# Linear attention and a gated long convolution on one core: keys and queries turned by crossbar transfers

## The chip, the cores and the metric

The kernel runs on one core of one Trainium2 chip. The metric is device time in microseconds (us), the median of several executions. A profile of one execution is taken beside it; its span is a little shorter than the time (280.3 against 282.08 us for the profiled run).

## The reference

Two stages, for 8 batches, 8 heads, a sequence of 576 and a head dimension of 64, with 128 random features. First, attention through positive random features:

```
scale = 1 / sqrt(sqrt(64));  q_s, k_s = q * scale, k * scale
phi(x): h = x @ omega.T - |x|^2 / 2;  exp(h - max(h)) / sqrt(128)
q_p, k_p = phi(q_s), phi(k_s)
kv = k_p^T v   (features x head dim, per batch and head);   z = sum over the sequence of k_p
attn = (q_p kv) / (q_p z + 1e-6)
```

Then its heads are put side by side (x: 576 x 512 a batch), and a gated convolution follows:

```
x1, x2, x3 = split(x @ w_proj)            # 512 -> 3 x 512
x2c = irfft(rfft(x2) * filter_fft), along the sequence
out = (x1 * x2c * x3) @ w_out             # float32, 8 x 576 x 512
```

## The kernel before

All of it is one program with everything in bf16 on TensorE. The sequence of 576 is cut into a main part of 512 (`NT` = 4 tiles of 128 rows) and a rest of 64; the rests of two batches share one tile of 128 rows ("left keys", "left queries", "left out").

**Attention, for each batch b.** GpSimd's queue loads `kn`, `qn` and `vn` (`load_main`, L430), 512 KB each in bf16 after the cast in the transfer, two buffers each. They come with the sequence on the partitions, while the feature matmuls need the head dimension there, so they have to be turned. `turn_keys` (L932) and `turn_queries` (L942) each work on half a batch: `transposes` (L818) runs eight 128x128 transposes on TensorE (matmuls against the identity `ident`) into the one PSUM bank `t`, and one copy takes the eight out of PSUM into half of `kt` or `qt`. Keys are copied by VectorE, queries by VectorE in batches 0 and 1 and by ScalarE from batch 2 on. `kt` and `qt` have one buffer each. Then `key_features` (L860) multiplies `kt` with `om2`, two heads' copies of omega on a block diagonal, and ScalarE's exponential writes `ek`; the stage "queries" does the same for `eqt`. "values" finds the maximum over the features and weighs the values with it; "sums" makes `kv` (with the normaliser as a 65th column), "turn out" multiplies `eqt` with it, normalises, and turns the result again (`turn_back`, into `xt`). For batches from `NS` = 2 on the queries are loaded in four pieces with the heads beside each other in a row of the sequence; batches 0 and 1 have another layout.

**The convolution.** The Fourier transform is a set of matmuls with tables of sines, on thirds of the sequence ("fold", "rest", "forward", "inverse"), the two gates are "gates", the last product "out". Between forward and inverse, the halves of `sp` are exchanged over the partitions by transfers on SyncE's queue (`sw<-sp`, and `xw<-xr` for the rest); that queue also stores the output. The filter's spectrum is made once ("filter") and spread by small transfers (`hps`, `hqs`).

**The order of work.** Nothing is issued as it is written. Each call is recorded by a planner (`Plan`); an operation has a due time, the batch number plus `LEAD` of its stage, plus `SHIFT` for some stages and batches, plus `LEAN` for some stages on some engines. A list scheduler with rough costs (`_cost`, L200) then walks through engines, buffers and transfer lanes (`simulate`) and among the operations that can start within 120 ns takes the one that is due first. The order it finds is issued (`issue`, L371), which is why nearly all rows of the profile stand at line 377. Each engine then works through its own queue in that order, and waits where an operand isn't there yet.

Of the kernel before, what the change touches and what calls it, by code (L numbers as in the profile page):

```python
# [20 lines left out]
P = 128  # L21

LEAD = {
    "filter": -1.47, "fold": 3.3, "forward": 1.54, "gates": 4.97, "inverse": -3.71, "keys": -2.66,
    "left keys": -4.9, "left out": -4.44, "left queries": -2.12, "load filter": -0.67,
    "load k": -2.73, "load kl": -3.56, "load q": -1.37, "load ql": 2.9, "load v": -2.25,
    "load vl": 1.29, "load w0": 1.23, "load w1": -2.06, "load w2": -0.52, "out": 3.79,
    "queries": 1.94, "residues": -0.5, "rest": -1.06, "sines": -0.54, "start": -3.3,
    "sums": -0.38, "tables": -3.64, "turn out": -3.39, "turn queries": -3.76, "values": 1.2,
    "zeros": -4.6,  # L30
}

SHIFT = {
    ("filter", 0): 2.36, ("fold", 2): -2.58, ("fold", 6): -3.0, ("forward", 1): 1.21,
    ("forward", 6): 1.02, ("forward", 7): 2.73, ("gates", 0): -0.44, ("gates", 1): -2.7,
    ("gates", 2): -1.54, ("gates", 6): 0.81, ("gates", 7): -2.03, ("keys", 1): 2.3,
    ("keys", 6): 2.62, ("keys", 7): -0.96, ("left keys", 2): 2.75, ("left out", 1): 2.97,
    ("left queries", 7): 1.34, ("load filter", 0): 0.55, ("load k", 0): 0.68, ("load k", 2): 2.87,
    ("load kl", 0): 1.02, ("load q", 0): 0.44, ("load q", 1): -3.0, ("load q", 2): -1.75,
    ("load ql", 0): -1.55, ("load v", 0): -2.22, ("load v", 1): -2.86, ("load v", 2): 2.32,  # L40
    ("load vl", 0): -1.68, ("load w0", 0): -2.48, ("load w1", 0): 2.15, ("load w2", 0): 0.69,
    ("out", 1): -2.05, ("out", 7): 2.04, ("rest", 1): -1.46, ("sines", 0): 2.98,
    ("start", 0): -2.92, ("sums", 7): 1.33, ("turn out", 0): -1.37, ("turn out", 1): -2.6,
    ("turn out", 2): -2.52, ("turn out", 7): -3.0, ("turn queries", 2): 2.54, ("values", 1): 1.63,
    ("values", 6): 3.0,
}
LEAN = {
    ("filter", "DVE"): -2.97, ("fold", "ACT"): -2.99, ("fold", "DVE"): -0.81,
    ("fold", "PE"): -1.4, ("forward", "ACT"): -3.0, ("forward", "DVE"): 2.93,
    ("forward", "PE"): 2.66, ("gates", "ACT"): -2.82, ("gates", "DVE"): -1.75,  # L50
    ("gates", "PE"): 2.18, ("keys", "DVE"): -2.89, ("keys", "PE"): -2.89,
    ("left keys", "DVE"): -1.5, ("left keys", "PE"): 2.06, ("left out", "ACT"): 2.24,
    ("left queries", "PE"): 1.68, ("out", "PE"): -0.68, ("queries", "ACT"): -1.85,
    ("queries", "PE"): -1.44, ("rest", "DVE"): -2.12, ("rest", "PE"): 2.72,
    ("start", "POOL"): 3.0, ("sums", "PE"): -3.0, ("turn out", "DVE"): 2.67,
    ("turn out", "PE"): 0.88, ("turn queries", "PE"): 0.32,
}

SIZE = {FP32: 4, INT32: 4, BF16: 2, FP16: 2, mybir.dt.uint32: 4}
# [57 lines left out]
class Plan:  # L117
# [82 lines left out]
    def _cost(self, op, eng, name, outs, ins):  # L200
        out = outs[0]
        n = self._free(out)
        if name == "dma_start":
            a = out if out.space != bass.MemoryType.DRAM else ins[0]
            run = a.ap[-1][1] * SIZE[a.dtype]
            rows = a.ap[0][1] * self._free(a) // a.ap[-1][1]
            if eng == "POOL":
                op.busy, op.lat = (880.0 if rows > 600 else 720.0), 3300.0
                op.dma = ("SW", rows * max(run, 166) / 198.0)
            else:  # L210
                op.busy, op.lat = 580.0, 2000.0
                op.dma = ("HW", rows * run / 180.0 / (1 if out.space == bass.MemoryType.DRAM else 4))
            return
        half = all(SIZE[a.dtype] == 2 for a in (out, *ins))
        sbuf = all(a.space != bass.MemoryType.PSUM for a in (out, *ins))
        if eng == "PE":
            m = n / 2.4 + 2.5
            op.lat = op.busy + n / 2.4 + 166.0
            op.busy += m
            return  # L220
        if eng == "DVE":
            if name == "memset":
                busy = n * SIZE[out.dtype] / 4.8 + 5.0
            elif name == "reciprocal":
                busy = 5.8 * n + 78.0
            elif name == "tensor_tensor":
                busy = n / (1.92 if half and sbuf else 0.96) + 68.0
            elif name == "scalar_tensor_tensor":
                busy = n / 0.96 + 130.0
            elif name in ("tensor_copy", "tensor_scalar", "tensor_scalar_mul"):  # L230
                rate = (4 if sbuf else 2) if half else (2 if sbuf else 1)
                if name != "tensor_copy" and not sbuf:
                    rate = 1
                busy = n / (0.96 * rate) + (68.0 if half else 100.0)
            elif name == "reduce_max":
                busy = self._free(ins[0]) / 0.96 + 60.0
            else:
                busy = n / 0.96 + 68.0
            op.busy, op.lat = busy, busy + 82.0
        elif eng == "ACT":  # L240
            busy = n * 0.8333 + (52.0 if not sbuf else 190.0)
            op.busy, op.lat = busy, busy + 107.0
        else:
            op.busy = op.lat = n / 1.2 + 100.0
# [136 lines left out]
def kernel(  # L381
# [11 lines left out]
    nc = Plan(tc.nc, tc)  # L393
# [5 lines left out]
    NS = 2  # L399
# [3 lines left out]
    NPAIR = H // 2  # L403
# [107 lines left out]
    for j in range(2):  # L511
        nc.vector.tensor_scalar_mul(
            out=om2[j * D : (j + 1) * D, j, :], in0=omt[:D, :MF], scalar1=qk_scale
# [34 lines left out]
    residues = {}  # L548
# [364 lines left out]
    def attention():  # L913
        ekl = None
        for i in range(B // 2):
# [5 lines left out]
            for bb in range(2):  # L921
                b = 2 * i + bb
# [3 lines left out]
                qn, kn, vn = (nat_tiles[w, b] for w in "qkv")  # L926


                kt = nc.tile(att, [P, H, 2, P], BF16, name="kt", bufs=1)
                qt = nc.tile(att, [P, NT, NPAIR, P], BF16, name="qt", bufs=1)  # L930

                def turn_keys(g):  # L932
                    transposes(
                        kt[:, 4 * g : 4 * g + 4, :, :].rearrange("p h u c -> p (h u) c"),
                        [
                            kn[:, h, 2 * u2 : 2 * u2 + 2, :].rearrange("p t d -> p (t d)")
                            for h in range(4 * g, 4 * g + 4)
                            for u2 in range(2)
                        ],
                    )  # L940

                def turn_queries(g):  # L942
                    transposes(
                        qt[:, 2 * g : 2 * g + 2].rearrange("p t h c -> p (t h) c"),
                        [
                            qn[:, t, 2 * pr : 2 * pr + 2, :].rearrange("p h d -> p (h d)")
                            for t in (2 * g, 2 * g + 1)
                            for pr in range(NPAIR)
                        ]
                        if b >= NS  # L950
                        else [

                            qn[:, h, 2 * u2 : 2 * u2 + 2, :].rearrange("p t d -> p (t d)")
                            for h in range(4 * g, 4 * g + 4)
                            for u2 in range(2)
                        ],
                        b >= 2,
                    )

                def turn_left(dst, src, scalar=False):  # L960
# [27 lines left out]
                if b == 0:  # L988
                    nc.at("residues", 0)
                    make_residues()  # L990
                    nc.at("zeros", 0)
                    nc.vector.memset(vcl[:], 0.0)
                    nc.vector.memset(eql[:], 0.0)
                nc.at("keys", b)
                ek = nc.tile(att, [P, H, NT, MF], BF16, name="ek", bufs=2)
                for g in range(2):

                    turn_keys(g)
                    for h in (4 * g, 4 * g + 2):
                        key_features(  # L1000
                            ek[:, h : h + 2, :, :].rearrange("p h t m -> p (h t m)"),
                            [kt[:, hh, u2, :] for hh in (h, h + 1) for u2 in range(2)],
                        )
# [20 lines left out]
                    left_keys()  # L1024
                nc.at("turn queries", b)
                for g in range(2):
                    turn_queries(g)
                nc.at("values", b)
                weigh_values()

# [2 lines left out]
                for pr in range(NPAIR):  # L1033
                    ps = two_banks()
                    for j in range(2):
                        nc.tensor.matmul(
                            out=ps[:, j, :],
# [4 lines left out]
                            start=True,  # L1042
# [3 lines left out]
                        out=eqt[:, pr].rearrange("p j t c -> p j (t c)")  # L1046
                        if b >= NS
                        else eqt[:, pr].rearrange("p h (u j) c -> p j (h u) c", j=2),
                        in_=ps[:] if b >= NS else ps[:].rearrange("p j (g c) -> p j g c", c=P),
# [440 lines left out]
```

The softmax here doesn't subtract the row's maximum and nothing guards it: scores larger than these inputs give would overflow.

## Time and profile before

| what | value |
|---|---|
| time, median of 3 | 282.09 us (280.8 to 282.12) |
| span of the profiled execution | 280.3 us |
| TensorE clock granted | 0.998 of full |
| VectorE, ScalarE, GpSimd busy | 229.9, 201.4, 62.5 us |
| packets of GpSimd's transfers | 59,616, 17.31 MB |
| packets of SyncE's transfers | 8,280, 12.75 MB |
| HBM read, written | 34.64 MB, 9.44 MB |

A row of the profile names line, engine, operation, the tile written and the tiles read, the shape and the count; behind the bar stand the busy time in us, the mean of one in ns, then the idle time of the engine just before such an instruction and what ended it. `t<-ident,kn` is a transpose of keys on TensorE, `kt<-t` its copy out of PSUM. PE is TensorE, DVE VectorE, ACT ScalarE, POOL GpSimd. Records of matmuls are longer than the distance from one to the next, since matmuls are pipelined.

### The profile page before, as it was taken

How to read it: one execution, taken by the hardware profiler on the slowest of the kernel's cores; microseconds unless marked ns; L12 is line 12 of the kernel's file. 1: busy time of each engine (PE TensorE's matmuls, PEld its weight loads, DVE VectorE, ACT ScalarE, POOL GpSimd, SP SyncE). 2: the span in 40 equal slices, each digit the busy share in tenths (PEclk: the TensorE clock that was granted, in tenths of full speed). 3: DMA queues.
4: the chain of work that ended last, by engine and by line, in shares of the span. 5: the costliest groups of instructions: out<-in, count | busy, mean ns of one | idle time of the engine just before them, and what ended most of it. 6: DMA issues, size and time to landing. Idle time of an engine off the chain costs nothing.

```text
span 280.3 us, 5836 instructions
## 1 busy us (share of the span) xinstructions
PE 255.7 (91%) x2274; PEld 156.2 (56%) x2274; DVE 229.9 (82%) x501; ACT 201.4 (72%) x309; POOL 62.5 (22%) x86
## 2 busy tenths in 40 slices
PE   0276797999999999999999999999999999999994
PEld 0154554666686765667566565586455555454541
DVE  7879986757969999999999999978999456776840
ACT  1877577798669797889998979948855656464443
POOL 8725766623127310062031000000000000000000
PEclk9999999999999999999999999999999999999999
DMA  7999999999599981369319022003002213033135
GB/s 90 188 201 191 165 199 187 207 185 117 52 167 173 127 107 26 115 84 169 67 26 223 27 77 87 37 21 77 1 2 112 78 39 132 37 115 102 47 116 187
DMA packets 68068, 30.56 MB, mean 109 GB/s; under 512 B 39499, under 2 KB 62536, under 8 KB 68040
## 3 DMA queue, kind: packets, MB, share of 16 engines
q0 software_dynamic: 59616, 17.31, 60.0%
q1 hardware_dynamic: 8280, 12.75, 14.6%
q8 instruction: 18, 0.29, 0.4%
q10 hardware_dynamic: 144, 0.13, 0.1%
q14 instruction: 10, 0.08, 0.1%
HBM read 34.64 MB, written 9.44 MB: 157 GB/s over the span
## 4 chain that ended last, share of the span: by engine, by line
PE 65%; DMA 17%; issue 9%; POOL 4%; DVE 3%; ACT 0%; DVEq 0%; POOLq 0%
PE h L377 49%; PE a L377 11%; PE t L377 5%; DMA vn<-in_v_dram 5%; DMA vl<-in_v_dram 5%; DMA ql<-in_q_dram 4%; DMA qn<-in_q_dram 3%; POOL qn L377 2%; POOL ql L377 1%; DVE vcl L377 1%; DMA out_dram<-x 1%; POOL vn L377 1%; POOL kl L377 0%; DVE sp L377 0%; POOL vl L377 0%
## 5 line engine op out<-in xcount | busy, mean ns | idle before, releaser
L377 PE MATMUL h<-xt,wproj 128*128 128x512 bf16 x256 | 61.4, 379 | 0.0
L377 ACT CAST x<-h 128x512 bf16<-128x512 f32 x68 | 40.4, 607 | 24.9 <-PE h L377 22.2
L377 PEld LDWEIGHTS <-wproj 128*128 128x128 bf16 x384 | 31.9, 98 | 25.5 <-issue 0.3
L377 ACT ACTIVATE eqt<-a 128x1024 bf16<-128x1024 f32 x32 | 32.5, 1051 | 6.1 <-PE a L377 6.1
L377 ACT ACTIVATE ek<-a 128x1024 bf16<-128x1024 f32 x32 | 32.2, 1039 | 4.0 <-PE a L377 4.0
L377 DVE TENSOR_TENSOR x<-h,x 128x512 bf16<-128x512 f32 x32 | 22.0, 687 | 15.6 <-PE h L377 15.3
L377 ACT ACTIVATE osb<-h 128x512 f32<-128x512 f32 (+3 forms) x46 | 26.2, 571 | 8.9 <-PE h L377 7.0
L377 POOL DMA_DIRECT2D qn<-in_q_dram x26 | 22.9, 894 | 41.0 <-PE t L377 35.8
L377 PE MATMUL h<-wout,yt 128*128 128x512 bf16 x128 | 31.6, 379 | 0.3 <-DVE yt L377 0.3
L377 PE MATMUL h<-wproj,xf 128*128 128x512 bf16 x128 | 31.4, 379 | 0.1
L377 DVE TENSOR_TENSOR xb<-a,rden 128x512 bf16<-128x512 f32 x36 | 24.9, 691 | 1.2
L377 PE MATMUL a<-om,kt 128*128 128x256 bf16 x128 | 18.1, 276 | 2.8 <-DVE kt L377 2.6
L377 PEld LDWEIGHTS <-yt 128*128 128x128 bf16 x128 | 12.0, 98 | 13.2 <-DVE yt L377 0.8
L377 PE MATMUL h<-x,fwb 128*128 128x512 bf16 x72 | 19.3, 379 | 0.0
L377 PEld LDWEIGHTS <-xf 128*128 128x128 bf16 x134 | 12.5, 98 | 12.1 <-DVE xf L377 0.5
L377 PE MATMUL a<-qt,om 128*128 128x512 bf16 x64 | 18.2, 381 | 0.7 <-DVE xb L377 0.4
L377 DVE TENSOR_TENSOR bt<-h,osb 128x384 f16<-128x384 f32 x32 | 16.6, 552 | 2.6 <-PE h L377 2.6
L377 PEld LDWEIGHTS <-kt 128*128 128x128 bf16 x128 | 12.1, 99 | 8.3 <-DVE kt L377 4.1
L377 PE MATMUL h<-gtab,xs 128*128 128x384 bf16 x64 | 15.6, 326 | 0.0
L377 ACT CAST sp<-h 128x512 bf16<-128x512 f32 x16 | 9.1, 591 | 7.8 <-PE h L377 7.8
L377 PE MATMUL t<-ident,xb 128*128 128x128 bf16 x144 | 13.8, 238 | 0.0
L377 PEld LDWEIGHTS <-xb 128*128 128x128 bf16 x144 | 10.7, 102 | 5.3 <-DVE xb L377 0.9
(168 smaller groups left out, 516.4 us busy)
## 6 DMA issues: line engine op xcount, KB each, us to landing
out_dram<-osb SPq DMA_DIRECT2D x24, 256.0 KB, 2.0
vn<-in_v_dram POOLq DMA_DIRECT2D x8, 512.0 KB, 7.5
kn<-in_k_dram POOLq DMA_DIRECT2D x7, 512.0 KB, 6.9
qn<-in_q_dram POOLq DMA_DIRECT2D x24, 128.0 KB, 6.9
sw<-sp SPq DMA_DIRECT2D x16, 128.0 KB, 3.5
wproj<-in_moe_w_proj_dram POOLq DMA_DIRECT2D x3, 512.0 KB, 11.1
qn<-in_q_dram POOLq DMA_DIRECT2D x2, 512.0 KB, 13.7
out_dram<-xf SPq DMA_DIRECT2D x4, 256.0 KB, 2.6
```

The costliest lines, as they stand in the source:

```text
L377: getattr(real, name)(*args, **kw)
```

## The change

From batch 2 on (`crossed = b >= NS`) the keys and the queries of a batch are each turned by one transfer through the crossbar of the DMA engines, issued on SyncE's queue, from `kn` straight to `kt` and from `qn` to `qt`, 512 KB each. The eight-fold transposes on TensorE, the PSUM bank they pass through and the copies on VectorE and ScalarE are left out for these batches; batches 0 and 1 keep them. It is meant to take work off the three compute engines and give it to transfers.

Two stages are new to the planner ("cross keys", "cross queries"), and it gets a cost for such a transfer. The tables `LEAD`, `SHIFT` and `LEAN` are replaced as a whole, so the order of all work, the loads included, is another. In the order that results, GpSimd's queue begins with queries of batch 0, a third of `wproj`, the left keys, a second third of `wproj`, the left values, half the keys of batch 0, the keys of batch 1, and the other half of batch 0 (before: the values of batches 0 and 1, the left keys, the keys of batches 0 and 1, a third of `wproj`, the queries). SyncE's queue begins with omega, keys 2, queries 2, queries 3, keys 3, and only then the first exchange `sw<-sp`. On TensorE the filter's transform moves from before the first gates into the middle of the forward transform of batch 1, and attention's stages of batches 2 and 3 come earlier against the convolution.

```diff
@@ LEAD, SHIFT, LEAN: all values replaced, of which
+    "cross keys": -12.62, "cross queries": -3.44, "filter": -12.92, "fold": -22.17,
...
@@ _cost
+        if name == "dma_start_transpose":
+            op.busy, op.lat = 580.0, 2000.0
+            op.dma = ("HW", self._free(out) * 128 * 2 / 175.0)
+            return
@@ attention
+                crossed = b >= NS
+
+                def cross(dst, src):
+                    nc.sync.dma_start_transpose(out=dst, in_=src)
...
                 def turn_queries(g):
                     transposes(
                         qt[:, 2 * g : 2 * g + 2].rearrange("p t h c -> p (t h) c"),
                         [
-                            qn[:, t, 2 * pr : 2 * pr + 2, :].rearrange("p h d -> p (h d)")
-                            for t in (2 * g, 2 * g + 1)
-                            for pr in range(NPAIR)
-                        ]
-                        if b >= NS
-                        else [
-
                             qn[:, h, 2 * u2 : 2 * u2 + 2, :].rearrange("p t d -> p (t d)")
                             for h in range(4 * g, 4 * g + 4)
                             for u2 in range(2)
                         ],
-                        b >= 2,
                     )
...
+                if crossed:
+                    nc.at("cross keys", b)
+                    cross(
+                        kt[:].rearrange("p h u c -> p (h u) c"),
+                        kn[:].rearrange("p h t d -> p (h t d)"),
+                    )
+                    nc.at("cross queries", b)
+                    cross(
+                        qt[:].rearrange("p t h c -> p (t h) c"),
+                        qn[:].rearrange("p t h d -> p (t h d)"),
+                    )
                 nc.at("keys", b)
...
                 for g in range(2):
-                    turn_keys(g)
+                    if not crossed:
+                        turn_keys(g)
...
                 for g in range(2):
-                    turn_queries(g)
+                    if not crossed:
+                        turn_queries(g)
```

## The prediction

> **What bounds the kernel now.** I read the busy shares first, then the windows by stage, then the order of time on TensorE, then the groups that the change touches, then the transfers. The first line names a candidate and proves nothing, as a busy matmul record is not a matmul at full rate.
>
> ```profile
> PE 255.7 (91%) x2274; PEld 156.2 (56%) x2274; DVE 229.9 (82%) x501; ACT 201.4 (72%) x309; POOL 62.5 (22%) x86
> ```
>
> The windows (length, then busy time of PE, PEld, DVE, ACT, POOL, then the granted clock, the DMA share, and GB/s) show where TensorE's missing time lies: before 49 us and in the last twenty.
>
> ```profile
> 7.00:14.00 7.00, 1.85 (x13) 1.36 (x14) 5.92 (x16) 5.70 (x10) 5.60 (x8) 1.00 1.55 188
> 42.00:49.00 7.00, 5.47 (x60) 3.09 (x58) 4.82 (x9) 5.26 (x9) 4.70 (x6) 1.00 2.00 187
> 49.00:56.00 7.00, 7.00 (x90) 4.82 (x87) 5.14 (x11) 4.91 (x9) 4.74 (x6) 1.00 1.44 207
> 110.00:120.00 10.00, 10.00 (x96) 5.96 (x95) 9.61 (x23) 7.30 (x12) 0.00 (x0) 1.00 0.26 94
> 160.00:180.00 20.00, 20.00 (x167) 11.90 (x165) 19.20 (x45) 18.30 (x28) 0.00 (x0) 1.00 0.24 79
> 260.00:280.30 20.30, 16.39 (x80) 7.46 (x78) 9.37 (x19) 8.37 (x15) 0.00 (x0) 0.98 0.35 117
> ```
>
> To see whether "10.00 of 10" is full rate, I take TensorE's instructions in order of time and read the distance from one start to the next, not the length of a record (records overlap).
>
> ```profile
> 100.90 0.61 PE L377 MATMUL t<-ident,kn 128*128 128x128 bf16 x8
> 101.35 0.59 PE L377 MATMUL a<-qt,om 128*128 128x512 bf16 x2
> ...
> 111.09 1.02 PE L377 MATMUL h<-wout,yt 128*128 128x512 bf16 x4
> 111.95 0.39 PE L377 MATMUL t<-ident,xb 128*128 128x128 bf16 x4
> 112.18 1.03 PE L377 MATMUL h<-wout,yt 128*128 128x512 bf16 x4
> ```
>
> Four matmuls of 512 columns take 111.95 - 111.09 = 0.86 us, 0.42 ns a column; four transposes of 128 columns take 0.23 us, 0.45 ns a column. I then added the columns of all matmuls window by window at 0.42 ns. From 49 to 260 us they come to 95 to 102% of each window: TensorE streams without holes. The whole program is about 248 us of streaming in a span of 280.3, so some 32 us are lost, and by window 26 of them lie before 49 us (22.6 us of streaming there) and 4 to 5 after 260. So each column taken out after 49 us shortens the run by its own time, until something else ends last. VectorE (19.2 of 20) and ScalarE (18.3 of 20) are near, but not first. Before 49 us loads set the pace: about 190 GB/s in every window, and the chain there is made of loads.
>
> **What the Trainium skill says.** "VectorE: DVE Perf Modes", section on the three transpose paths, gives 390 ns for a 128x128 transpose on TensorE and 1309 ns on the crossbar. The trace disagrees with the first as a cost in a stream: records of 219 ns, but 0.45 us for eight. No run here shows the second yet. "DMA: Bandwidth & Descriptors", section on issuing engines, says that transfers from every issuing engine share the same 16 DMA engines; the trace agrees, since 64 KB of hps issued by SyncE amid the loads takes 6.4 us to land, and 256 KB to the output, late and alone, 2.0.
>
> **The change, part by part.** It removes, in batches 2 to 7, two groups of eight key transposes and two of eight query transposes each: 24 groups. These are the rows concerned.
>
> ```profile
> L377 PE MATMUL t<-ident,kn 128*128 128x128 bf16 x128 | 10.2, 225 | 0.5 <-DVE qt L377 0.5
> L377 PE MATMUL t<-ident,qn 128*128 128x128 bf16 x128 | 9.7, 219 | 1.7 <-DVE qt L377 1.4 <-DMA x<-in_moe_filter_fft_dram 0.2
> L377 DVE COPY kt<-t 128x1024 bf16<-128x1024 bf16 x16 | 11.0, 684 | 0.6 <-PE t L377 0.5
> L377 ACT COPY qt<-t 128x1024 bf16<-128x1024 bf16 x12 | 12.6, 1046 | 0.3 <-PE t L377 0.2
> ```
>
> TensorE: the busy column (10.2 + 9.7 us for 256) counts pipeline tails and the slow first batches. In the stretch from 60 us on, each group of eight moves the next start by 0.44 to 0.45 us. 24 x 0.445 = 10.7 us, all but the first group or two inside the full stretch, so on the path: **-10.7 us**.
>
> Copies: VectorE loses 12 x 0.684 = 8.2 us, ScalarE 12.6 us. Both lie beside the full TensorE, so **0 us** directly; they buy slack where both were over 90% busy, which has little to win, as TensorE lost only about 1.5 us between 49 and 260.
>
> Added: 12 crossbar transfers of 512 KB on SyncE's queue. The trace has none, so I bound one. Lower end: "DMA: Bandwidth & Descriptors", section on latency and other measured facts, has 261 GB/s for a transpose with a non-contiguous middle dimension, and its section on the anatomy of one DMA about 2.0 us fixed (the trace's 256 KB stores agree with the latter): 524 KB / 261 = 2.0, so an estimate of 4 us alone. Upper end: if every 128-element row is a packet (256 bytes, 2048 of them) at the 45 ns that the loads' 59,616 packets show (60.0% of 16 engines x 280.3 us), 5.8 us of all engines; with the other half of the engines' turns going to loads, about 12 us, which is also twice the 6.4 us that hps needed under load. I take 5 us after 110 us, where the DMA share is small, and 8 us before.
>
> The added waits: kt and qt have one buffer each. A transfer for batch b waits for the last matmul that reads batch b-1, and the first matmul of b, with all of TensorE's in-order queue behind it, waits for its landing. Walking the changed order with 0.42 ns a column, the streaming work between these two points is 10.2, 26, 8.5, 8.2 and 11.3 us for the keys of batches 3 to 7, and 24, 25, 18, 7.9 and 25 us for the queries. All are above 5 us, so after 110 us the transfers are hidden by the matmuls of the gates, inverse and output stages: **0 us**. On SyncE, a spectrum exchange (sw) and stores are queued behind a waiting transfer; the trace shows sw landing in 3.5 us with only 0.6 us waited for it, and the transposes stand ahead of the exchanges only where TensorE does their readers' work first, so 0.
>
> The tables that set the order are new too, so the loads come in another order: queries of batch 0 and two thirds of wproj first, keys of batch 0 behind them, the filter late. Up to the first key half that is about 2 MB on the SBUF side instead of 1.4 MB, so its first matmul comes about 3 us later, while queries(0), 1.7 us of streaming plus turns, is done before it. kn of batch 2 is about 5.6 MB in: 30 us at 190 GB/s plus the 4 us by which the trace's first keys trail such a sum, 34 us. Its transfer lands at 42 by my 8 us, the queries' behind it at 46 to 50; the new order asks for the former after 17 us of streaming and for the latter after 21. The old order had 17.5 us streamed at 42 us and 22.6 at 49. So I charge the front **+2 us** (0 to 6).
>
> Sum: 282.09 - 10.7 + 2 = **273.4 us**.
>
> **The rivals.**
> *(1) The waits take the gain back.* For it: one buffer, one in-order queue, DMA engines full until 105 us, covers of only 8 us. With 12 us a transfer, five covers fall short by 1.8 + 3.5 + 3.8 + 0.7 + 4.1 = 14 us, and the front by 4 more: 282.1 - 10.7 + 18 = 289, slower. Against it: after 110 us the DMA share is 0.1 to 1.2, and a transfer alone should take near 4.
> *(2) A partial loss.* Transfers of 9 to 10 us, or one load in the front that comes 6 us late: 282.1 - 10.7 + 8 = 279.5.
> *(3) The new order also mends the front.* Of the 26 us lost there, 5 are won because TensorE gets queries(0) early and less waits on VectorE's copies: 282.1 - 10.7 - 5 = 266.4. For it: VectorE is busy for 36 of the first 42 us. Against it: the first keys come later.
>
> **How the numbers follow.** 0.62 for the forecast (about 269 to 277), 0.13 for (3), 0.14 for (2), 0.11 for (1). The range takes in the upper price of the early transfers and most of (3): 266.5 to 280.0, leaving out about 2 in 10. Faster by more than 0.5% (below 280.7): 0.85; within: 0.05; slower: 0.10.
>
> **What would show each step right or wrong.** Right: the groups t<-kn and t<-qn fall from x128 to x32, streaming from about 50 us to the end stays within 5% of full, and the sum of columns is 10 us smaller. Copies: DVE busy down by about 8 us and ACT by 12. Transfers: landing of kt and qt under 8 us after 110 us, and no more than 1 us that PE waits for them in all. Front: the stretch before full rate ends near 50 us. Wrong: long waits of PE for DMA kt or qt (rival 1), SyncE's exchanges late and VectorE waiting for sw, or PE's first full window later than 55 us (rival 2) or earlier than 45 (rival 3).

## The result and the profile after

| | before | after |
|---|---|---|
| time, median of its runs | 281.83 us (280.8 to 282.12) | 292.36 us (291.89 to 293.08) |
| span of the profiled execution | 280.3 us | 290.4 us |
| VectorE, ScalarE busy | 229.9, 201.4 us | 222.7, 195.7 us |

The ratio is 1.0383, with a 95% interval of 1.0347 to 1.0418: slower, where 273.4 us and a gain were forecast. Executions more than 1.5% slower than the fastest of the same kernel are left out of the times and ratios below (5 of 20 in plain_copy, one of 4 in dummy_cross4).

These rows are from the page of the changed kernel: busy time with the count of instructions, then the granted TensorE clock and the mean share of the DMA engines in 40 slices of 7.3 us.

```profile
PE 252.6 (87%) x2049; PEld 149.3 (51%) x2082; DVE 222.7 (77%) x489; ACT 195.7 (67%) x299; POOL 62.6 (22%) x86
PEclk9998978799996999999999999999999999999999
DMA  7999999999999369497995993343420021311325
```

The weight loads fall from 2274 to 2082, 192 fewer: the 24 groups of eight. (PE shows 2049, since some records of matmuls are missing; the weight loads, one for each matmul, are complete.) The DMA row reads 9 until about 95 us, and the clock reads below 9 (90%) in five of the first 13 slices, where it was 1.00 in every window to 100 us of the kernel before.

The windows of the changed kernel (columns as in the prediction), with one of the kernel before as the last row, show where the time went.

```profile
42.00:49.00 7.00, 3.44 (x57) 2.77 (x55) 1.34 (x3) 4.14 (x6) 1.56 (x2) 0.95 1.46 136
49.00:56.00 7.00, 6.55 (x50) 4.09 (x52) 3.57 (x11) 2.20 (x3) 3.21 (x5) 0.56 1.88 159
80.00:90.00 10.00, 4.20 (x40) 2.37 (x40) 2.84 (x8) 2.77 (x5) 3.96 (x5) 0.79 1.57 189
160.00:180.00 20.00, 19.64 (x150) 11.61 (x150) 18.91 (x45) 16.61 (x26) 2.67 (x4) 1.00 1.21 113
...
80.00:90.00 10.00, 10.00 (x130) 7.56 (x128) 9.71 (x19) 7.35 (x12) 5.74 (x7) 1.00 1.43 174
```

Between 80 and 90 us TensorE is busy for 4.2 of 10 us, where it was busy throughout before, while the transfer engines have at least as much to do (a share of 1.57 against 1.43). A share above 1 means that the records of packets overlap: two packets that are under way on one engine both count. Late in the run (160 to 180) nothing is wrong. To put a number on it, I take the matmuls in program order, give each its columns at 0.42 ns, and use the count of weight loads that had started by a given time to say how much of the program was streamed by then. What is lost is the time less the work streamed. All such sums, here and below, come from the one profiled execution of a kernel and are good to about half a us.

| us | before | after | difference |
|---|---|---|---|
| streaming in the whole program | 241.5 | 231.2 | -10.3 |
| streamed by 100 us | 70.8 | 51.9 | |
| lost before 100 us | 29.2 | 48.1 | +18.9 |
| lost after 100 us | 9.6 | 11.1 | +1.5 |
| span | 280.3 | 290.4 | +10.1 |

Until 35 us the two are equal within that. So the gain on TensorE came, all 10.3 us of it, and nearly twice as much was lost while the loads were still coming in.

The rows that answer to the removed work, from the groups of the changed kernel:

```profile
L375 PE MATMUL t<-ident,kn 128*128 128x128 bf16 x32 | 2.9, 242 | 0.0
L375 DVE COPY kt<-t 128x1024 bf16<-128x1024 bf16 x4 | 2.7, 687 | 2.4 <-PE t L375 2.4
L375 DVE COPY qt<-t 128x1024 bf16<-128x1024 bf16 x4 | 2.7, 682 | 0.0
```

And the added work, from its tables of queues and of issues (queue: packets, MB, share of 16 engines; issue: count, KB, median us from issue to landing). The first row is SyncE's queue in the kernel before, the rest is from the changed one:

```profile
q1 hardware_dynamic: 8280, 12.75, 14.6%
...
q1 hardware_dynamic: 33240, 19.04, 29.9%
...
vn<-in_v_dram POOLq DMA_DIRECT2D x8, 512.0 KB, 11.0
kn<-in_k_dram POOLq DMA_DIRECT2D x7, 512.0 KB, 10.3
...
kt<-kn SPq DMA_TRANSPOSE x6, 9.4
qt<-qn SPq DMA_TRANSPOSE x6, 10.9
```

By the records of their packets the twelve transfers thus took (0.299 x 290.4 - 0.146 x 280.3) / 12 = 3.83 us each, counted over **all sixteen** engines, in (33,240 - 8,280) / 12 = 2,080 packets. As records overlap where two queues are busy, this is a price and not the time for which a transfer has the engines to itself, and it depends on the traffic. The same row of SyncE's queue between 37 and 79 us, where the first four transfers move, and between 130 and 134 us, where one moves nearly alone:

```profile
q1 hardware_dynamic: 8322, 2.10, 42.3%
...
q1 hardware_dynamic: 2080, 0.52, 71.7%
```

That is 0.423 x 42 = 17.8 us for the four, 4.4 each, and 0.717 x 4 = 2.87 us for the one. The loads land later too: a load of 512 KB of keys took 6.9 us to land before and 10.3 now, one of values 7.5 and 11.0. But in plain_copy below, which is as fast as the kernel before, they take 9.1 and 10.1, so these medians don't show where the time went.

### The profile page after: what moved, and what is told of

Same layout as the page of the kernel before. It is cut to its first block, busy times and chain, and to the rows that moved or that the text cites. A ratio compares the mean times of both kernels' runs of the same rounds, so it can differ in the third digit from the quotient of the medians.

```text
span 290.4 us, 5421 instructions
## 1 busy us (share of the span) xinstructions
PE 252.6 (87%) x2049; PEld 149.3 (51%) x2082; DVE 222.7 (77%) x489; ACT 195.7 (67%) x299; POOL 62.6 (22%) x86
## 3 DMA queue, kind: packets, MB, share of 16 engines
q1 hardware_dynamic: 33240, 19.04, 29.9%
## 4 chain that ended last, share of the span: by engine, by line
PE 49%; DMA 18%; DVE 11%; issue 10%; ACT 8%; POOL 2%; SPq 0%; DVEq 0%; POOLq 0%; ACTq 0%
PE h L375 39%; PE a L375 8%; DMA kt<-kn 7%; DMA qt<-qn 4%; DMA yt<-in_moe_filter_fft_dram 4%; DMA vn<-in_v_dram 3%; PE t L375 2%; ACT eqt L375 2%; ACT L375 2%; DVE x L375 1%; DVE h L375 1%; POOL qn L375 1%; DVE vcl L375 1%; DMA xw<-xr 1%; ACT ek L375 1%
## 5 line engine op out<-in xcount | busy, mean ns | idle before, releaser
L375 ACT CAST x<-h 128x512 bf16<-128x512 f32 x68 | 39.8, 598 | 26.2 <-PE h L375 26.2
L375 PE MATMUL h<-wout,yt 128*128 128x512 bf16 x122 | 30.4, 379 | 0.6 <-DVE yt L375 0.3
L375 PE MATMUL h<-wproj,xf 128*128 128x512 bf16 x123 | 29.6, 379 | 0.3
L375 PE MATMUL a<-om,kt 128*128 128x256 bf16 x128 | 20.4, 290 | 6.8 <-DMA kt<-kn 3.9
L375 PE MATMUL a<-qt,om 128*128 128x512 bf16 x62 | 19.8, 419 | 0.6 <-DVE xb L375 0.6
L375 PE MATMUL a<-kv,eqt 128*128 128x65 bf16 x256 | 13.4, 202 | 7.2 <-DVE xb L375 6.6
L375 PEld LDWEIGHTS <-kt 128*128 128x128 bf16 x128 | 12.4, 103 | 13.1 <-DMA kt<-kn 4.3
L375 PE MATMUL h<-x,fwb 128*128 128x512 bf16 x66 | 18.4, 383 | 0.5 <-issue 0.2
L375 PEld LDWEIGHTS <-yt 128*128 128x128 bf16 x128 | 11.8, 98 | 13.3 <-DVE yt L375 0.8
L375 PEld LDWEIGHTS <-eqt 128*128 128x128 bf16 x256 | 12.1, 104 | 11.8 <-DVE xb L375 7.9
L375 POOL DMA_DIRECT2D vn<-in_v_dram x8 | 7.1, 883 | 43.4 <-DVE vc L375 40.8
## 6 DMA issues: line engine op xcount, KB each, us to landing
kn<-in_k_dram POOLq DMA_DIRECT2D x7, 512.0 KB, 10.3
qn<-in_q_dram POOLq DMA_DIRECT2D x24, 128.0 KB, 10.1
```

Of the source, the lines that this page charges most:

```text
L375: getattr(real, name)(*args, **kw)
```

## The experiments

Two explanations stood against each other first. Theory A: the crossbar transfers cost the time, because they take the transfer engines from the loads that the front waits for. Theory B: the new tables put the loads in a worse order. Later runs tell, within A, the transfer engines' time from the wait of kt's or qt's readers for the landing.

### The order and the transfers apart

*order_only*: the code before, with `LEAD`, `SHIFT` and `LEAN` of the changed kernel; no crossbar transfer.

> The new tables, and with them the new order of loads and stages, but all keys and queries turned on TensorE with copies, as before. Theory A (the crossbar transfers cost the time: they land late while the loads fill the DMA engines, and the loads behind them land later too): without them the order is about as good as the old one, 280 to 286 us, TensorE waits for no transfer around 46 and 82 us. Theory B (the new order costs the time, the transfers save their 10.7 us): 300 us or more.

*cross_only*: the changed code, with the tables before. The two new stages need due times, and one load must come earlier:

```diff
+    "cross keys": -2.66, "cross queries": -3.76,
...
-    ("load k", 2): 2.87,
+    ("load k", 2): 0.0,
```

> The crossbar transfers from batch 2 on under the old tables (cross keys and cross queries get the due times of keys and turn queries, and one load, the keys of batch 2, is due earlier). Theory A: slower than before, 286 to 295 us, with transfers of batches 2 and 3 that land in 10 us or more and TensorE waiting for them. Theory B: about 272 us.

*cross_late_new* and *cross_late_old*: transfers from batch 4 on instead of 2, batches 0 to 3 turned on TensorE with the layouts and copies of the kernel before; once with the new tables, once with those of before (cross keys at -5.0, cross queries at -4.0).

```diff
-                crossed = b >= NS
+                crossed = b >= 4
```

> The changed kernel, but batches 2 and 3 are still turned on TensorE, and the crossbar takes over from batch 4, when the loads are mostly done. 16 groups less on TensorE than before, 7.1 us. Theory A: 275 to 282 us, no hole near 46 us. Theory B: over 290 us, since the order stays new.

> Old tables, crossbar from batch 4 on only. Both theories: about 275 us (282 less 16 groups of 0.445 us), unless late transfers cost as well; under theory A with long landings at any load, 278 to 284 us.

| kernel | tables | turned by transfers | time, us | ratio to before (95%) | lost by 100 us | lost after |
|---|---|---|---|---|---|---|
| before | old | none | 281.8 | | 29.2 | 9.6 |
| order_only | new | none | 315.11 | 1.1182 (1.1139 to 1.1226) | 36.7 | 35.7 |
| cross_only | old | from 2 | 305.6 | 1.0854 (1.0821 to 1.0886) | 52.4 | 20.2 |
| after | new | from 2 | 292.36 | 1.0383 (1.0347 to 1.0418) | 48.1 | 11.1 |
| cross_late_new | new | from 4 | 297.62 | 1.0562 (1.0508 to 1.0617) | 37.5 | 23.7 |
| cross_late_old | old | from 4 | **277.63** | 0.9868 (0.9837 to 0.9898) | 29.1 | 13.0 |

Neither theory had this. The new tables without transfers are far worse, 315 us, and the transfers with the old tables are worse too, 306 us. The two changes are not a sum: with its own operations each set of tables loses about 10 us after 100 us (9.6 and 11.1), but the new set without transfers loses 35.7 there and the old set with transfers from batch 2 loses 20.2. That is no rule, since the old set with transfers from batch 4 loses only 13.0. The column "lost by 100 us" is cleaner: within each set it follows the transfers. From batch 2 it is 48 and 52, from batch 4 it is 37.5 and 29.1, as without any (36.7 and 29.2). The new tables lose 7.5 us more than the old ones even without a transfer, but not in the stretch of the loads: counted in the same way at 90 us, order_only is 1.8 us behind the kernel before, and the rest is lost between 90 and 100 us, after 20 us in which its transfer engines had a share of 0.46 and 0.60. With the old tables, beginning at batch 2 costs 23 us of the front (more than the 17.8 us of four transfers' packets: a single wait of TensorE for kt is 7.4 us of it, and one load was moved), and beginning at batch 4 costs nothing there. That is also the version that beats both kernels, by 1.3% against before.

### The crossbar or the bytes

*plain_copy*: the changed kernel with the twelve transfers as plain ones of the same 512 KB, the planner's cost kept, so that every engine's order is the same. Keys and queries of batches 2 to 7 are copied and not turned.

```diff
-                    nc.sync.dma_start_transpose(out=dst, in_=src)
+                    nc.sync.dma_start(out=dst.rearrange("p g c -> p (g c)"), in_=src)
```

> The changed kernel with every crossbar transfer replaced by a plain transfer of the same 512 KB from kn to kt and from qn to qt, in the same place of the same queue and with the same waits; keys and queries of batches 2 to 7 are then not turned, so this part of the computation is left out. All engines' orders stay as they are. If the transfer's own length in the DMA engines under load is what hurts (2080 packets of 256 bytes each, landing in 9 to 15 us): plain transfers have a few hundred packets, land in 3 to 6 us, and the time falls to 278 to 285 us. If waiting on any transfer between load and use is what hurts, or the order itself: 289 to 293 us.

Measured: 281.21 us, 0.999 (0.9969 to 1.0011) of before. 34.8 us are lost before 100 us and 12.5 after; against the changed kernel, 13.3 us less before and 1.4 more after. From its page:

```profile
PEclk9999999999999999999999999999999999999999
...
q1 hardware_dynamic: 10008, 19.04, 20.6%
...
kt<-kn SPq DMA_DIRECT2D x6, 512.0 KB, 4.2
qt<-qn SPq DMA_DIRECT2D x6, 512.0 KB, 6.6
```

The same bytes in (10,008 - 8,280) / 12 = 144 packets, and (0.206 x 278.5 - 0.146 x 280.3) / 12 = 1.37 us of packets' time each: 2.46 us less than through the crossbar. As both kernels' load queues hold the same loads in the same order, I can follow one load through the two. First the changed kernel's GpSimd queue in order of time (start, length, what, and the idle time before it):

```profile
46.21 0.88 POOL L375 DMA_DIRECT2D vn<-in_v_dram  x1 [2.42 <-DMA ql<-in_q_dram]
...
50.56 0.88 POOL L375 DMA_DIRECT2D kn<-in_k_dram  x1 [0.17 <-issue]
...
60.83 0.69 POOL L375 DMA_DIRECT2D vl<-in_v_dram  x1 [0.53 <-DMA kl<-in_k_dram]
...
72.36 3.58 POOL L375 DMA_DIRECT2D qn<-in_q_dram  x4 [2.38 <-DMA qt<-qn]
75.90 1.11 POOL L375 DMA_DIRECT2D yt<-in_moe_filter_fft_dram  x2
...
80.06 0.94 POOL L375 DMA_DIRECT2D kn<-in_k_dram  x1 [2.43 <-DMA kt<-kn]
...
86.57 0.76 POOL L375 DMA_DIRECT2D wout<-in_moe_w_out_dram  x1
```

Then the same six loads (without the qn) in plain_copy:

```profile
44.20 0.88 POOL L377 DMA_DIRECT2D vn<-in_v_dram  x1 [0.17 <-issue]
...
48.16 0.88 POOL L377 DMA_DIRECT2D kn<-in_k_dram  x1 [0.57 <-DMA ql<-in_q_dram]
...
55.33 0.70 POOL L377 DMA_DIRECT2D vl<-in_v_dram  x1
...
68.29 1.08 POOL L377 DMA_DIRECT2D yt<-in_moe_filter_fft_dram  x2 [0.33 <-DMA yt<-in_moe_filter_fft_dram]
...
70.28 0.94 POOL L377 DMA_DIRECT2D kn<-in_k_dram  x1 [0.29 <-DMA x<-in_moe_filter_fft_dram]
...
74.04 0.77 POOL L377 DMA_DIRECT2D wout<-in_moe_w_out_dram  x1 [0.52 <-DMA qn<-in_q_dram]
```

The lateness grows step by step: 2.0 us at vn, 2.4, 5.5, 7.6, 9.8 at kn, 12.5 at wout. Four transfers lie before the load of kn. Their packets took 17.8 us in the changed kernel, and in plain_copy, between 37 and 68 us, 0.186 x 31 = 5.8 us:

```profile
q1 hardware_dynamic: 576, 2.10, 18.6%
```

The difference of 12.0 us is near the 9.8 to 12.5 us by which the loads are late. But the 13.3 us of TensorE are not the loads' lateness alone. Against plain_copy the changed kernel has lost 5.4 us by 56 us, 6.1 by 80, 11.8 by 90 and 13.1 by 100 (counted in the same way): two steps. The second, at 80 to 100 us, is the hole of the late loads. The first is a wait for a transfer to land, with a low clock after it (0.56 for 49 to 56 us, above). The matmul in question in the changed kernel, and in plain_copy, where it doesn't wait:

```profile
49.23 1.04 PE L375 MATMUL a<-om,kt 128*128 128x256 bf16 x4 [3.31 <-DMA kt<-kn]
...
44.98 0.64 PE L377 MATMUL a<-om,kt 128*128 128x256 bf16 x4
```

Not all of the lateness need be packets' time either: the notes in brackets show GpSimd's queue itself waiting 2.4 us twice for a transfer to have read `qn` or `kn` before the buffer may be loaded again, with all later loads queued behind. At 72 us loads issued earlier were still on their way, so such a wait may cost less than its length; how much isn't separated.

*filter_first*: the changed kernel with the filter's loads (`yt`, `x`) issued ahead of the queries of batches 4 and 5, as VectorE's longest wait there was for the filter.

```diff
+        at = next(i for i, o in enumerate(ops) if o.eng == "POOL" and o.where == ("load q", 4))
+        late = [o for o in ops[at:] if o.eng == "POOL" and o.where == ("load filter", 0) and "wout" not in o.name]
+        ops = ops[:at] + late + [o for o in ops[at:] if o not in late]
```

> The changed kernel, in which GpSimd issues the filter's loads before the queries of batches 4 and 5, which wait for the buffers that the crossbar transfers free; nothing else moves. If the hole near 82 us (TensorE waits for VectorE, which waits for the filter) comes from this queueing, VectorE's wait for the filter (9.5 us) goes, and the time falls by 4 to 8 us, to 284 to 288 us. If the hole has another cause or its time is lost elsewhere: within 1.5 us of 292.

Measured: 292.56 us, 1.0411 (1.0396 to 1.0427), no gain. In the changed kernel's timeline TensorE stood still for the filter's chain, by way of VectorE: first TensorE, then VectorE.

```profile
88.39 0.62 PE L375 MATMUL a<-kv,eqt 128*128 128x65 bf16 x8 [5.75 <-DVE xb L375]
```

```profile
87.06 0.42 DVE L375 TENSOR_TENSOR yt<-yt 128x512 bf16<-128x512 bf16 x1 [7.33 <-DMA yt<-in_moe_filter_fft_dram]
```

In filter_first's timeline VectorE waits at nearly the same place for another load:

```profile
83.58 0.87 DVE L379 TENSOR_TENSOR vcl<-vl,vcl 64x512 bf16<-64x512 bf16 x2 [9.92 <-DMA vl<-in_v_dram]
```

The queue as a whole is late, and moving one load forward moved the hole to one that was overtaken. The wait at 87 us was the place where the loss showed, not its cause.

### The displacement by itself

*dummy_cross4*: the kernel before, with four crossbar transfers added at the start, from the values of batches 0 and 1 to a spare buffer that nothing reads. *dummy_plain4*: the same with four plain ones. All other work is kept in its order.

```diff
+                if b < 2:
+                    nc.at("start", b)
+                    src = vn[:].rearrange("p h t d -> p (h t d)")
+                    spare = nc.tile(hy, [P, 16, P], BF16, name="x13", bufs=3)
+                    for _ in range(2):
+                        nc.sync.dma_start_transpose(out=spare[:], in_=src)
```

> The kernel before, unchanged in all it computes, with four crossbar transfers of 512 KB added on SyncE's queue between 10 and 45 us (from vn of batches 0 and 1 to a free buffer that nobody reads). No engine's order moves and nothing on TensorE waits for them. If the transfers hurt by taking the DMA engines from the loads (3.8 us of all 16 engines each): the loads, and with them the first stage, come later by up to 15 us, and the time is 288 to 297 us. If they hurt only where TensorE waits for their landing: 281 to 283 us.

> As the run with four unread crossbar transfers, but with four plain transfers of the same bytes (1.4 us of all engines each). If taking the DMA engines from the loads is what counts: 284 to 288 us, about a third of the other's loss. If bytes alone count, the same loss as the crossbar's; if only waits for landing count: 281 to 283 us.

| kernel | time, us | ratio to before (95%) | lost by 100 us, over before | the four transfers' packets |
|---|---|---|---|---|
| dummy_cross4 | 298.24 | 1.0596 (1.0529 to 1.0662) | +14.7 | 0.198 x 295.3 - 40.9 = 17.6 us |
| dummy_plain4 | 287.33 | 1.0189 (1.0173 to 1.0206) | +4.7 | 0.164 x 285.4 - 40.9 = 5.9 us |

The last column is from SyncE's queue in the two, less its 0.146 x 280.3 = 40.9 us before:

```profile
q1 hardware_dynamic: 16600, 14.85, 19.8%
...
q1 hardware_dynamic: 8856, 14.85, 16.4%
```

No matmul waits for these transfers, and the planner's tables are untouched; the front loses 0.84 and 0.80 of what their packets take. After 100 us the two lose 9.9 and 10.0 us, as before (9.6). The profiled execution of dummy_cross4 (297.1 us) was its fastest, so the usual loss is about 1 us larger, a little more than expected. What TensorE waits longer for are loads: 5.5 us for `ql` (1.5 before) and 2.6 for `qn` (none before). SyncE's queue is also held by the transfers, and the first `hps` goes out at 49.3 us instead of 40.0, but TensorE's wait for the stage behind it (`yt`, 0.3 us) is as before. Again one load can be followed through GpSimd's queue; its place before, with four crossbar transfers, and with four plain ones:

```profile
54.86 0.69 POOL L377 DMA_DIRECT2D vl<-in_v_dram  x1 [0.66 <-DMA vn<-in_v_dram]
```

```profile
68.98 0.72 POOL L380 DMA_DIRECT2D vl<-in_v_dram  x1
```

```profile
59.84 0.69 POOL L380 DMA_DIRECT2D vl<-in_v_dram  x1 [0.90 <-DMA vn<-in_v_dram]
```

Late by 14.1 and 5.0 us, the same as TensorE's loss within 0.6 us. (Not all of the 14.1 must come straight from the transfer engines: a group of loads a little earlier waited 2.9 us for TensorE to free its buffer, and TensorE was late too.)

### How early may the transfers start

Four more kernels with the old tables vary the batch from which the transfers are used; the edit is as in cross_late_old (`b >= 3`, `b >= 5`), or with one condition for keys and one for queries.

> Old tables; only the queries take the crossbar, from batch 4 on, and all keys stay on TensorE: 8 groups less than before, 3.6 us. The late transfers of keys showed two waits of TensorE (1.1 and 1.3 us) when keys and queries both crossed from batch 4; without them 277 to 279 us. If keys are not what cost there: 279 to 281 us.

> Old tables; queries cross from batch 4 on, keys from batch 6 on: 12 groups less than before, 5.3 us. If the loss of the late transfers lies in the keys of batches 4 and 5, which cross amid the last loads: 275.5 to 277 us. If each transfer costs alike: 277 to 279 us.

> Old tables, crossbar from batch 3 on (20 groups, 8.9 us less on TensorE). If what counts is how many crossbar transfers fall into the loads: between the 277.6 us of batch 4 on and the 305.6 us of batch 2 on, 280 to 292 us. If batch 2 alone was the trouble: 273 to 276 us.

> Old tables, crossbar from batch 5 on (12 groups, 5.3 us less on TensorE). If the loss with batch 4 on (3.3 us against full gain) comes from transfers that meet the last loads, a smaller loss here: 276 to 278 us. If each transfer costs alike: 278 to 279.5 us.

| kernel | turned by transfers | time, us | ratio to before (95%) | streaming | lost by 100 us | lost after |
|---|---|---|---|---|---|---|
| cross_from3_old | from 3 | 287.45 | 1.0178 (1.0141 to 1.0214) | 232.9 | 29.1 | 23.6 |
| cross_late_old | from 4 | 277.63 | 0.9868 (0.9837 to 0.9898) | 234.7 | 29.1 | 13.0 |
| cross_from5_old | from 5 | 280.68 | 0.9983 (0.9958 to 1.0007) | 236.4 | 29.6 | 15.5 |
| late_q4_k6 | queries 4, keys 6 | 279.22 | 0.9935 (0.9918 to 0.9951) | 236.4 | 29.2 | 11.9 |
| late_q4_k8 | queries from 4 | 279.87 | 0.9955 (0.9935 to 0.9976) | 238.1 | 28.5 | 11.2 |

The front is unharmed in all five. What they lose after 100 us differs by 12 us and isn't in proportion to the count of transfers: fewer of them (from 5) lose no less than from 4. (The profiled executions of cross_from5_old and cross_late_old took 2.6 and 1.0 us longer than the medians, so their usual losses are nearer 12.9 and 12.0 us.) Compare one window of cross_from3_old,

```profile
110.00:120.00 10.00, 7.37 (x93) 4.90 (x92) 9.76 (x24) 6.50 (x10) 0.88 (x1) 1.00 1.09 177
```

with the same window of cross_late_old:

```profile
110.00:120.00 10.00, 9.89 (x106) 5.85 (x105) 9.67 (x21) 8.34 (x12) 3.80 (x5) 1.00 1.90 198
```

VectorE is as busy in both (9.76 and 9.67 of 10) and the clock is full, but TensorE has 7.37 in one and 9.89 in the other, although the transfer engines are fuller in the better one. This points to the order of VectorE's work and away from the transfers; it wasn't tested by itself. The planner, with tables made for other work, finds another order for each set, and why one costs 2 to 3 us more than its neighbour stays open. About half of TensorE's gain or less arrives in the time: streaming falls by 3.4, 5.1 and 6.8 us in late_q4_k8, late_q4_k6 and cross_late_old, and the ratios make it 1.3, 1.8 and 3.7 us; the rest is in "lost after", which was 9.6 before. The intervals of three of the five lie wholly below 1.

## Why the prediction was wrong

*TensorE's saving of 10.7 us: right.* The program's streaming fell by 10.3 us, and no new hole after 100 us took it back (+1.5 us).

*Copies at 0: right as far as it goes.* VectorE is busy for 7.2 us less, ScalarE for 5.7; the latter less than the 12.6 us of its copies, with five loads of activation tables at 1.28 us each in the new order, where there were three, among the causes. After 110 us TensorE waits for neither by more than 0.5 us.

*A transfer's landing, 5 us late and 8 us in the front: right alone, too low in the front.* At 129 and 189 us, with little beside them, a transfer lands in 4.3 us, near the 4 us that were estimated, though not as they were split: 2.0 us for the bytes and 2.0 fixed, where the packets of one alone take 2.87 us, which leaves 1.4. The 2.0 us fixed of the Trainium skill ("DMA: Bandwidth & Descriptors", section on the anatomy of one DMA) are stated there for transfers that GpSimd issues, and these are SyncE's; nor did the trace agree, as a 256 KB store takes 2.0 us with its bytes. After 110 us most land in 4.3 to 5.1 us, one (at 158 us) in 10.3. The first four took 15.2, 12.5, 11.0 and 12.9 us, and the first of these made TensorE wait: it was to land at 42 us and landed at 49.

*Waits after 110 us at 0: right.* From the waits of the changed kernel (total, times, longest): TensorE waits for kt twice, both times before 110 us, the longer at 49 us.

```profile
PE a L375 <- DMA kt<-kn: 3.9, 2, 3.3
```

*The front at +2 us (0 to 6): this is the step that failed.* It measured +18.9 us. I asked when each transfer would land and whether its reader had enough work as cover, and charged nothing for the time that the transfers take from the loads, though the same text had "loads set the pace: about 190 GB/s in every window" and had quoted the skill that all queues share the sixteen engines. The numbers were there: an upper end of "5.8 us of all engines" for one transfer, used for its landing only. The packets of the four transfers that move before 79 us took 17.8 us among the loads; four like them that nothing reads (dummy_cross4) cost the front 14.7 us, and the loads of the changed kernel come up to 12.5 us later than those of plain_copy. The landing itself was put too low as well: the 3.3 us wait at 46 us, and the clock after it, stand in the first step of the loss.

How the 18.9 us divide is known in part. With every engine's order kept, plain transfers in place of the crossbar's bring 13.3 us of them back, 5.4 in the first step and most of the others in the second. Of the remaining 5.6 us, 4.7 is what four plain transfers cost in dummy_plain4, which leaves next to nothing for the new order of loads; that is an estimate from these runs, in line with order_only, which is 1.8 us behind at 90 us.

*Rival 1's 289 us came near, by the wrong road.* It had waits of TensorE for landings, 14 us of them after the front. They were 3.9 us in all, none after 110 us; the larger part of the loss went with the late loads, before 100 us.

*The loss to start from was mis-sized.* "32 us lost, 26 before 49 us" counted groups at window edges twice in the streaming (248 us). By program order it is 241.5 us of streaming and 38.8 us lost in the kernel before: about 27 of them before 49 us, 2 from there to 100 us and 9.6 after. The loss in the front was thus nearly right, and what was missed lies after 100 us.

What stays open is the clock. After the 3.3 us wait at 46 us the granted clock is 0.56 for 49 to 56 us, and the mean over the run is 0.965, against 0.998 before and 1.000 in plain_copy. The Trainium skill, "TensorE: Matmul & The Clock Gate", part 1 on the HAM clock gate, says that an idle window of about 3.4 us halves the clock; the drop after this wait of 3.3 us agrees. Summing busy TensorE time times the missing clock over the windows to 100 us gives about 7.5 us, 2.9 of them from 49 to 56 us. Work that waits for loads anyway doesn't feel it, and in dummy_cross4 the loads' lateness matches the loss within 0.6 us while the clock fell as far (0.960). But in the front the lower clock came together with late loads, so how much of the loss is the clock's own isn't shown. A second buffer for kt and qt wasn't tried.

## What to carry to other kernels

Before moving work to transfers, ask which stretch is bound by transfers, and price each new one there by the time it takes from the other transfers as well as by its landing and who waits for it: the twelve transfers saved TensorE 10 us, and the front, where four of them fell among the loads, lost 19, of which 13 come back when the same bytes go as plain transfers. The same transfers are worth having once the loads have thinned out: from batch 4 on they win 1.3%, though from batch 5 on, in the order that the planner then finds, nothing (0.9983, interval 0.9958 to 1.0007). And an order that a planner was tuned to for one set of operations is not a constant to carry to another set: after 100 us the new tables lost 26 us more without the transfers than the old ones (order_only), the old ones 11 us more with transfers from batch 2 than with none (cross_only), and 3 us more with transfers from batch 4.

## What the runs showed of the hardware

A crossbar transfer of 512 KB in bf16 from SBUF to SBUF, sixteen 128x128 blocks, is 2,080 packets. Nearly alone (130 to 134 us of the changed kernel) their records add up to 2.87 us of all sixteen engines (524 KB / 2.87 us = 183 GB/s), 22 ns a packet on one engine (2.87 us x 16 / 2,080); over all twelve it is 3.83 us, and among the loads 4.4. The plain transfer of the same bytes takes 1.37 us over all twelve, and 0.439 x 3 = 1.32 us alone, between 166 and 169 us of plain_copy:

```profile
q1 hardware_dynamic: 144, 0.52, 43.9%
```

The Trainium skill, "Advanced Engine Details and Errata", section "X-Bar Transpose (TRN2)", has transposes as fast as regular transfers; here the crossbar takes 2.2 times as long alone and 2.8 times over all twelve, and the measurement decides.

The issue of one is long as well. SyncE's queue in the changed kernel, in order of time:

```profile
33.95 5.85 SPq L375 DMA_TRANSPOSE kt<-kn  x1
...
66.62 6.77 SPq L375 DMA_TRANSPOSE kt<-kn  x1
...
189.15 1.77 SPq L375 DMA_TRANSPOSE qt<-qn  x1
```

The same line of plain_copy takes a tenth of that:

```profile
33.85 0.56 SPq L377 DMA_DIRECT2D kt<-kn  x1
```

So the queue is held for 1.8 us when the engines are free and up to 6.8 us among the loads, and whatever stands behind it on that queue is issued later.
